# Linear attention and a gated MLP on one core: every SBUF tile moved by 32 bytes

## The chip, the core and the metric

The kernel runs on one core of one Trainium2 chip. The metric is the device time of one execution in microseconds; the time before the change is the median of three runs, 1343.54 us (1341.47 to 1345.01). One further execution was taken with the hardware profiler, and all trace numbers come from it. "PE" is TensorE's matmul stream, "PEld" the loading of its stationary operand, DVE is VectorE, ACT is ScalarE, POOL is GpSimd, and SP is the queue that starts most DMAs.

## The reference

```python
def phi(x):                                   # q, k, v: (8, 8, 576, 64); w_phi: (64, 128)
    proj = np.einsum('bhsd,df->bhsf', x, w_phi)
    proj = proj - np.max(np.abs(proj), axis=-1, keepdims=True)
    return np.concatenate([np.exp(proj), np.exp(-proj)], axis=-1)
q_p, k_p = (phi(q), phi(k))
kv = np.einsum('bhsf,bhsd->bhfd', k_p, v)
num = np.einsum('bhsf,bhfd->bhsd', q_p, kv)
den = np.einsum('bhsf,bhf->bhs', q_p, np.sum(k_p, axis=2))[..., None] + 1e-06
x = (num / den).transpose(0, 2, 1, 3).reshape(4608, 512)
xn = x / np.sqrt(np.mean(x * x, axis=-1, keepdims=True) + 1e-06) * rms_g
g = xn @ w_gate                               # w_gate, w_val: (512, 1536)
out = ((g / (1.0 + np.exp(-g))) * (xn @ w_val)) @ w_out     # w_out: (1536, 512)
```

All data are float32.

## The kernel before

Nearly all products are written as three matmuls of a split operand: a tile is rounded to float32r by ScalarE ("high") and the rest is kept in a second float32r tile ("low"), and high by high, high by low and low by high are added in PSUM. One matmul instruction takes a moving operand of N columns (128 partitions by N elements of 4 bytes, from SBUF) and a stationary operand of 128 columns that is loaded ahead of it (PEld). Three stages follow each other:

- **Attention, up to 508 us.** The 32 pairs of heads are worked off in a software pipeline (`front`, `mid`, `back`, `last`). `front` transposes k and q (L298) and projects them (L311 to L313, N = 256, moving `wh` or `wl`); `mid` exponentiates and forms kv (L346, N = 130, moving `vr`; L351, N = 65, moving `vm`; both in plain float32, which the trace shows as two matmuls for each that the code writes); `back` multiplies with the queries (L415, N = 288, moving `qh` or `ql`, 32 x 4 x 6 = 768 matmuls). Tiles `vm` and `vr` exist three times; pair number modulo 3 picks one. Between these, the first 3 of 12 column blocks of gate and value weights are multiplied with blocks of 288 tokens (`fill`, L474, N = 288, moving `xo`, 1152 matmuls), and go on alone until 606 us.
- **Gate and value, 611 to 1067 us.** For 12 blocks of 384 tokens the other 9 column blocks are multiplied (`gv`, L588, N = 384, moving `xb`, 12 x 9 x 24 = 2592 matmuls); L156 and L157 add 24 of the same width for the norm.
- **Output, 1075 to 1340 us.** For 18 groups of 256 tokens, seven products of a Strassen scheme are made (`omm`, L737, N = 256, moving `wh0` to `wh5` and `wl0` to `wl5`, stationary `xo`). A product runs over kp = 0 to 5, with three matmuls each (moving `wh`, `wl`, `wh`): 18 x 7 x 18 = 2268 matmuls.

Pools hand out SBUF from the low end of a partition, or, with `side="right"`, from the high end, and round each tile's size up to a multiple of 32 bytes. Byte addresses within the partition, as the built program has them:

| tiles | operand in | address of the first | modulo 64 |
|---|---|---|---|
| `eps`, `g` (pool `gl`) | - | 16512, 16544 | 0, 32 |
| `one`, `epsd`, `warm`, `ones` (pool `gl`) | L156 (`ones`) | 16576, 16608, 16640, 16672 | 0, 32, 0, 32 |
| `fg0` to `fv1` (wf1) | L474, L588, stationary | 17184 | 32 |
| `xb`, three buffers | L588, moving | 52512, 79136, 91424 | 32 |
| `xo` of `fill` | L474, moving | 153120, 162336 | 32 |
| `qh`, `ql` | L415, moving | 177696, 196128 | 32 |
| `wh`, `wl` | L311 to L313, moving | 135008, 136032 | 32 |
| `vm0`, `vm1`, `vm2` | L351, moving | 137056, 139136, 141216 | 32, 0, 32 |
| `vr0`, `vr1`, `vr2` | L346, moving | 143296, 143840, 144384 | 0, 32, 0 |
| `wh0` to `wl3` (pool `rg`, right side) | L737, moving | 172000 | 32 |
| `wh4` to `wl5` (pool `owp`, left side) | L737, moving | 113440 | 32 |
| `xo` of `operands` | L737, stationary | 64288 and 15 more | 32 |

All other tiles that TensorE reads (weights, `kt`, `qt`, `th`, `tl`, `er`, `ek`, `yk`, `yq`, `kv`, `ident`) also start at 32 modulo 64. Within a tile the slices that are passed to TensorE are multiples of 64 bytes apart, with `vm` and `vr` as the exception: the 65 columns of `vm` are 260 bytes apart.

The Tile framework sets the order of the instructions on each engine from the order in the code and its own estimates; all five engines run their rows in that order and wait on semaphores.

Of the kernel before, what the change touches and what calls it, by code (L numbers as in the profile page):

```python
# [8 lines left out]
F32 = mybir.dt.float32  # L9
# [73 lines left out]
def kernel(ctx: ExitStack, tc: tile.TileContext, q, k, v, w_phi,  # L83
# [29 lines left out]
    gl = ctx.enter_context(tc.tile_pool(name="gl", bufs=1))  # L113
# [3 lines left out]

    x_ctx = ExitStack()  # L120
    wfp = x_ctx.enter_context(tc.tile_pool(name="wfp", bufs=1))
    wf1 = [[wfp.tile([128, NC, J1 * 128], F32R, name=f"f{n}{i}") for i in range(2)] for n in "gv"]
# [678 lines left out]
```

## Time and profile before

| | |
|---|---|
| median of three runs | 1343.54 us |
| lowest and highest | 1341.47, 1345.01 us |
| span of the profiled execution, first to last instruction | 1345.4 us |
| matmuls in it | 9396 |
| TensorE waits in it for other work, longest sum by line | 9.8 us (L474 for DVE) |

The profiled execution's span lies 1.9 us above the median and 0.4 us above the slowest of the three runs. In the profile a row such as "2.24 PE L588 MATMUL ... x12" is a run of 12 like instructions, with the time from the first one's start to the last one's end. Matmuls overlap at their ends, so the pace of a stream is read from the starts of two runs that follow each other, not from the duration of one.

### The profile page before, as it was taken

To read this page: it belongs to the slowest core of one execution; us is meant where nothing else is said; L and a number is where in the kernel's file an instruction comes from. 1 tells how busy PE (TensorE), PEld (TensorE's weight loads), DVE (VectorE), ACT (ScalarE), POOL (GpSimd) and SP (SyncE) were. 2 spreads that over 40 slices of the span, in tenths; PEclk is the share of its full clock that TensorE was granted. 3 is DMA by queue.
4 is the path that set the end of the run, shared out by engine and by line. 5 is a ranking of instruction groups with operands and counts; after the bars stand their busy time and mean duration, and the time that the engine had idled before them with its cause. 6 is when DMAs were issued, how large, how long until landed. Compare 5 with 4: busy or idle time off the path is not lost.

```text
span 1345.4 us, 25468 instructions
## 1 busy us (share of the span) xinstructions
PE 1291.3 (96%) x9396; PEld 1275.3 (95%) x9396; DVE 914.7 (68%) x1301; ACT 710.0 (53%) x1510; POOL 619.6 (46%) x568
## 2 busy tenths in 40 slices
PE   7989999999999997998999999999999799999998
PEld 7889899999999887998999999999999799999998
DVE  7899888778778762114566656655343489999995
ACT  5988877778778772334434434443332234344332
POOL 3766565555556660000223222222221078878885
PEclk9999999999999898999999999999999999999999
DMA  5455656565556434437454454454333434454351
GB/s 162 125 144 158 162 159 166 168 170 167 161 151 162 125 113 144 150 128 203 145 171 145 157 176 154 133 169 151 110 123 100 158 116 136 132 172 137 126 176 60
DMA packets 204523, 197.21 MB, mean 147 GB/s; under 512 B 69553, under 2 KB 186417, under 8 KB 204401
## 3 DMA queue, kind: packets, MB, share of 16 engines
q1 hardware_dynamic: 194896, 190.88, 47.0%
q10 hardware_dynamic: 9504, 4.72, 1.2%
q8 instruction: 74, 1.21, 0.4%
q14 instruction: 49, 0.39, 0.1%
HBM read 126.04 MB, written 69.50 MB: 145 GB/s over the span
## 4 chain that ended last, share of the span: by engine, by line
PE 80%; DVE 7%; DMA 5%; ACT 4%; issue 2%; POOL 2%; SPq 0%; ACTq 0%; DVEq 0%; POOLq 0%
PE fp L588 15%; PE gp L588 15%; PE fp L474 10%; PE acc L351 6%; PE gd L737 5%; PE gz L737 5%; PE gy L737 5%; PE sm L415 3%; PE fp L737 2%; PE pp L311 2%; PE fp L415 2%; PE pp L313 2%; PE pp L312 2%; PE sm L298 2%; PE sm L364 2%
## 5 line engine op out<-in xcount | busy, mean ns | idle before, releaser
L380 POOL TENSOR_TENSOR ql<-eq,qh 128x256 fp32r<-128x256 f32 x256 | 217.1, 879 | 67.2 <-issue 38.2
L61 POOL TENSOR_TENSOR xo<-st,xo 128x768 fp32r<-128x768 f32 x54 | 125.0, 2328 | 94.0 <-ACT xo L60 92.2
L588 PE MATMUL fp<-xb,wg 128*128 128x384 f32 x864 | 163.0, 336 | 4.6 <-ACT wg L60 4.6
L588 PE MATMUL gp<-xb,wv 128*128 128x384 f32 x864 | 161.5, 334 | 0.0
L588 PEld LDWEIGHTS fp<-xb,wg 128*128 128x128 f32 x864 | 151.9, 189 | 5.1 <-ACT wg L60 4.9
L573 DVE TENSOR_TENSOR h<-sl,gp 128x384 f32<-128x384 f32 x108 | 59.5, 551 | 135.0 <-PE gp L588 71.2
L588 PEld LDWEIGHTS gp<-xb,wv 128*128 128x128 f32 x864 | 150.8, 188 | 0.0
L571 ACT ACTIVATE sl<-fp 128x384 f32<-128x384 f32 x108 | 52.7, 489 | 167.4 <-PE fp L588 148.6
L54 POOL TENSOR_TENSOR wa<-raw,wa 128x192 f32<-128x192 f32 (+1 forms) x112 | 67.4, 622 | 159.5 <-issue 56.7
L351 PE MATMUL acc<-vm,ek 128*128 128x65 f32 x1024 | 131.6, 271 | 0.0
L315 DVE TENSOR_REDUCE mx<-pp 128x4 f32<-128x512 f32 (+1 forms) x160 | 100.5, 631 | 42.4 <-PE pp L313 41.1
L351 PEld LDWEIGHTS acc<-vm,ek 128*128 128x128 f32 x1024 | 127.8, 194 | 0.3 <-ACT ek L338 0.2
L60 ACT CAST xo<-st 128x768 fp32r<-128x768 f32 x54 | 43.4, 835 | 153.1 <-DVE st L675 76.9
L61 POOL TENSOR_TENSOR xb<-x,xb 128x1536 fp32r<-128x1536 f32 x12 | 42.7, 3562 | 152.0 <-ACT xb L60 152.0
L151 POOL TENSOR_TENSOR ss<-ss,sq 128x384 f32<-128x384 f32 x36 | 37.5, 1041 | 154.4 <-ACT sq L150 154.4
L474 PE MATMUL fp<-xo,fg 128*128 128x288 f32 x576 | 95.9, 303 | 9.8 <-DVE xo L61 9.8
L376 ACT ACTIVATE qh<-sm 128x512 fp32r<-128x512 f32 (+1 forms) x192 | 97.1, 506 | 0.0
L474 PEld LDWEIGHTS fp<-xo,fg 128*128 128x128 f32 x576 | 81.8, 190 | 13.2 <-DVE xo L61 12.2
L474 PE MATMUL fp<-xo,fv 128*128 128x288 f32 x576 | 92.5, 299 | 0.0
L61 POOL TENSOR_TENSOR xo<-ht,xo 128x768 fp32r<-128x768 f32 x36 | 91.6, 2545 | 0.0
L311 PE MATMUL pp<-wh,th 128*128 128x256 f32 x288 | 88.6, 309 | 2.7 <-DVE yr L318 2.1
L375 ACT ACTIVATE eq<-sm 128x512 f32<-128x512 f32 x128 | 78.2, 611 | 13.1 <-PE sm L364 12.0
(163 smaller groups left out, 3589.1 us busy)
## 6 DMA issues: line engine op xcount, KB each, us to landing
hs<-h SPq DMA_DIRECT2D x144, 192.0 KB
ht<-hs SPq DMA_DIRECT2D x18, 1536.0 KB
gvs<-fo SPq DMA_DIRECT2D x96, 144.0 KB
gvr<-gvs SPq DMA_DIRECT2D x36, 384.0 KB
rc<-di SPq DMA_DIRECT2D x32, 288.0 KB
x<-xs SPq DMA_DIRECT2D x16, 576.0 KB
x<-xs SPq DMA_DIRECT2D x12, 768.0 KB
kt<-in_k_dram SPq DMA_DIRECT2D x32, 256.0 KB
```

Of the source, the lines that this page charges most:

```text
L54: nc.gpsimd.tensor_tensor(a[:, h], lf[:, h], a[:, h], ALU.mult)
L61: (lo_eng or nc.vector).tensor_tensor(lo, x, hi.bitcast(F32), ALU.subtract)
L311: nc.tensor.matmul(o, th[:, cs], wh, start=True, stop=False)
L315: nc.vector.tensor_reduce(mx[:, 0:2 * m], pp[:, 0:2 * m], axis=AX.X, op=ALU.max, apply_absolute_value=True)
L351: nc.tensor.matmul(acc[:, sg, h], e[h][:, sg, j], vm[:, h, j], start=False, stop=(h == 1 and j == T0 - 1))
L375: nc.scalar.activation(ei[:, sg], yi, AF.Exp, scale=1.0 - 2.0 * sg)
L376: nc.scalar.activation(hi[:, sg], yi, AF.Exp, scale=1.0 - 2.0 * sg)
L380: nc.gpsimd.tensor_tensor(lo[:, sg, cs], ei[:, sg, cs], hi[:, sg, cs].bitcast(F32), ALU.subtract)
L415: nc.tensor.matmul(o[:, 0:SH], a[:, h, sg], e[:, sg, h, cs], start=(i == 0), stop=(i == 5))
L474: nc.tensor.matmul(fp[:, 0:TF], w, xx[x][:, c], start=(i == 0), stop=(i == 3 * NC - 1))
L588: nc.tensor.matmul(gp[:, 0:T], w, e[:, c], start=(i == 0), stop=(i == 3 * NC - 1))
L737: nc.tensor.matmul(place[n], a[:, kp], w[:, o], start=(first and kp == 0 and i == 0), stop=(kp == KP - 1 and i == 2), skip_group_check=True)
```

## The change

Three lines are added after the first tiles of pool `gl`. A tile of 128 x 8 float32 is 32 bytes in each partition. The first call moves everything that the left side hands out later up by 32 bytes; the other two open a pool on the right side ahead of `rg`, and move everything there down by 32 bytes. The two new tiles are never written or read.

```diff
     g = gl.tile([128, NC], F32, name="g")
+    gl.tile([128, 8], F32, name="shift")
+    rsh = ctx.enter_context(tc.tile_pool(name="rsh", bufs=1, side="right"))
+    rsh.tile([128, 8], F32, name="shift")
     x_ctx = ExitStack()
     wfp = x_ctx.enter_context(tc.tile_pool(name="wfp", bufs=1))
```

Each engine has the same instructions in the same order, with the same waits, as before; only addresses differ. Left-hand tiles go up by 32 (`fg0` 17184 to 17216, `xb` 52512 to 52544, `wh4` 113440 to 113472), right-hand ones down by 32 (`wh0` 172000 to 171968). All tiles at 32 modulo 64 come to lie at 0, and the few at 0 (`vm1`, `vr0`, `vr2`; and `one`, `warm` and one buffer of `mx`, which TensorE does not read) at 32. `eps` and `g` stay where they were. DRAM addresses of the inputs and scratch tensors are not touched by the new lines.

## The prediction

> **What bounds the kernel.** I read the page's busy shares first, then the chain of work that ended last, then three stretches, one from each stage.
>
> ```profile
> span 1345.4 us, 25468 instructions
> PE 1291.3 (96%) x9396; PEld 1275.3 (95%) x9396; DVE 914.7 (68%) x1301; ACT 710.0 (53%) x1510; POOL 619.6 (46%) x568
> PEclk9999999999999898999999999999999999999999
> PE 80%; DVE 7%; DMA 5%; ACT 4%; issue 2%; POOL 2%; SPq 0%; ACTq 0%; DVEq 0%; POOLq 0%
> ```
>
> TensorE is busy for 96% of the span, it is 80% of the chain that ended last, and its clock is granted in full in nearly every slice. By stretch (busy us of each engine, then clock, DMA share and GB/s):
>
> ```profile
> core 0: us, PE busy (x) PEld busy (x) DVE busy (x) ACT busy (x) POOL busy (x), PEclk, DMA share, GB/s
> 200.00:400.00 200.00, 198.82 (x1646) 198.04 (x1645) 156.39 (x270) 152.83 (x382) 110.65 (x135) 1.00 0.60 166
> 700.00:800.00 100.00, 100.00 (x579) 100.00 (x578) 63.87 (x99) 42.14 (x74) 26.72 (x27) 1.00 0.50 157
> 1200.00:1300.00 100.00, 100.00 (x868) 100.00 (x867) 95.56 (x71) 39.57 (x58) 85.33 (x36) 1.00 0.46 148
> ```
>
> In each stage TensorE has no gap to speak of: 1.2 us of 200 in attention, none in the other two. So a change of TensorE's pace goes into the time nearly one for one, in both directions. The others have room (DVE at most 156 of 200 in attention, 64 of 100 in gate and value) except in the output stage, where DVE is busy for 95.56 of 100 us: TensorE cannot gain much over 4% there before DVE is the limit.
>
> The change adds no instruction, wait or transfer and moves none. What can differ is how long an instruction takes at its new address. So the sum has three parts: TensorE's pace at a start of 0 instead of 32 modulo 64; its pace where the distance between the two operands changes; and the other engines and DMAs.
>
> **1. The pace of the wide matmuls.** The starts of runs that follow each other, gate-and-value first, then `fill`:
>
> ```profile
> 699.68 2.24 PE L588 MATMUL gp<-xb,wv 128*128 128x384 f32 x12
> 701.76 2.24 PE L588 MATMUL fp<-xb,wg 128*128 128x384 f32 x12
> ...
> 570.15 1.76 PE L474 MATMUL fp<-xo,fv 128*128 128x288 f32 x12
> 571.75 1.76 PE L474 MATMUL fp<-xo,fg 128*128 128x288 f32 x12
> ```
>
> With N = 384, twelve take 701.76 - 699.68 = 2.08 us, 173.3 ns each. With N = 288 they take 1.60 us, 133.3 each. The difference of 40.0 ns for 96 columns is 0.417 ns for a column; by that the columns alone take 160.0 and 120.0 ns, and **13.3 ns** remain in both that do not depend on N. 16 columns take 6.67 ns, and 16 float32 are 64 bytes. If the remainder is two pieces of 64 bytes, one of them the piece that a start in the middle of 64 bytes adds (1536 bytes from offset 32 touch 25 such pieces, from offset 0 only 24), an aligned start saves 6.67 ns. If it is the change from one set of weights to the next, or loading and streaming getting in each other's way, it stays. No operand of a wide matmul starts at 0 now, so no row decides this directly; the bounds are zero and the whole remainder.
>
> How many there are: 2592 + 24 with N = 384, and 1152 + 768 with N = 288, 4536 in all. At nothing: 0. At one piece: 4536 x 6.67 ns = 30.3 us. At the whole remainder: 4536 x 13.3 = 60.5 us.
>
> The nearest row where offsets differ is in attention. `vm0` lies at 32 modulo 64 and `vm1` at 0, so by their pair numbers these two runs, with `vr` ahead of each, read the moving operand at both:
>
> ```profile
> 322.41 0.44 PE L346 MATMUL acc<-vr,er 128*128 128x130 f32 x2
> 322.69 1.90 PE L351 MATMUL acc<-vm,ek 128*128 128x65 f32 x16
> 324.42 0.39 PE L298 MATMUL sm<-ident,kt 128*128 128x128 f32 x2
> ...
> 433.56 0.44 PE L346 MATMUL acc<-vr,er 128*128 128x130 f32 x2
> 433.84 1.90 PE L351 MATMUL acc<-vm,ek 128*128 128x65 f32 x16
> 435.57 0.39 PE L298 MATMUL sm<-ident,kt 128*128 128x128 f32 x2
> ```
>
> The first is a pair with `vm0`, the second one with `vm1`: 324.42 - 322.69 and 435.57 - 433.84 are both 1.73 us, 108 ns a matmul, and `vr0` and `vr1` show 0.44 alike. So an aligned start gains nothing measurable there. The row is not strong: 65 columns are short beside 108 ns, which makes the loading of the weights the limit, and the stationary operands are at 32 in both. It does price the few tiles that go the other way (`vm1`, `vr0`, `vr2`) at nothing. I take 0 for the first part, and keep 30 us as the price of the rival.
>
> The Trainium skill speaks to both sides. Its page "SBUF — State Buffer" (Specifications) gives lines of 16 bytes; 32 modulo 64 is a line's start as much as 0 is, so by that rule the shift saves nothing, in agreement with the `vm` rows. Its page "TensorE: Matmul & The Clock Gate" (Back-to-back issue gap) gives N / 2.4 + 2.5 ns for a warm isolated stream, 162.5 for N = 384, where this trace has 173.3; if all that lies above the rule came from the offset, an estimate by that page is 10.8 ns x 4536 = 49 us.
>
> **2. The distance between the operands in the output stage.** Nearly all tiles move up together, so the distance between a matmul's moving operand and the weights loaded beside it stays. It changes in one place: `wh0` to `wl3` go down by 32 while the stationary `xo` go up by 32. Before, these are at 224 and `xo` at 32 modulo 256, 192 apart; after, 128 apart. `wh4` to `wl5` are 0 apart before and after. That this can matter is in the rows of the output stage (one product of 18, then the start of the next):
>
> ```profile
> 1201.52 0.28 PE L737 MATMUL gz<-wl,xo 128*128 128x256 f32 x1
> ...
> 1202.19 0.28 PE L737 MATMUL gz<-wl,xo 128*128 128x256 f32 x1
> ...
> 1202.54 0.27 PE L737 MATMUL gz<-wl,xo 128*128 128x256 f32 x1
> ...
> 1203.24 0.28 PE L737 MATMUL gz<-wl,xo 128*128 128x256 f32 x1
> ...
> 1113.60 4.16 PE gz L737 x36
> 1117.76 4.41 PE gd L737 x36
> ```
>
> Every third matmul reads a `wl`. From that of kp = 1 to that of kp = 3 (1201.52 to 1202.19) six matmuls, all with right-hand tiles, take 0.67 us, 112 ns each; from kp = 4 to kp = 0 of the next product (1202.54 to 1203.24) six, nearly all with left-hand tiles, take 0.70, 117 each. Size, type and stage are the same, so some address pattern above 64 bytes is worth 4 to 5 ns of a matmul. The last two rows come from the chain of waits: two products are 4.16 us to the next row, 115.6 ns a matmul on average.
>
> The right-hand matmuls are 18 x 7 x 12 = 1512. If all fall to 117 ns, that costs up to 1512 x 5 ns = 7.6 us; since the first of a product are slower than 112 already, I price it at 6 us. If the left-hand ones' slowness is not a matter of distance, it costs 0. If 128 were better than 192 it could gain, but 112 is near the 108 at which loading alone runs in the rows above: at most 1512 x 4 = 6 us. No row has 128 apart with N = 256. I take 0, between the two ends, and keep both.
>
> **3. The others.** DVE, ACT, POOL and the DMAs also get new addresses. In gate and value DVE could slow by half before it bound (63.87 of 100); in the output stage, at 95.56, it could slow by 4%. If that cover went, each further per cent of DVE there would cost about 2.7 us (1% of the stage's 266 us). No row says that they would be slower or faster: 0, both ways.
>
> **The sum.** 0 + 0 + 0 against the profiled execution's 1345.4 us; that lies 1.9 us above the median of the runs shown, so the prediction is made for the median: **1343.5 us**. With the small terms of part 2 in both directions the likeliest case alone spans 1338 to 1348.
>
> **Rivals.**
> - *A start at 64 bytes saves a piece.* Price 30 us, time 1343.5 - 30 = 1313; with something from the 256-wide matmuls as well (2268 of the output stage from 115.6 to at best 112, 8 us, which DVE's share allows) about 1305; at half the price 1328. For it speaks that the remainder is the same 13.3 ns in two widths and just 32 columns long, twice 64 bytes, while every operand starts mid-piece. Against it speak the `vm` rows, and that a change of weights would give the same constant. At the whole remainder 1283.
> - *Slower through the distance.* The mechanism of part 2 in the output stage: 1343.5 + 6 = about 1350; it becomes visible once the 1512 right-hand matmuls lose over 2.7 ns each (4 us). For it: 112 beside 117 ns. Against it: the wide matmuls show one pace although the blocks of `xo` in `fill` lie at four distances from their weights. The same page on TensorE (Step-by-step) says that moving operand and weights have two independent read ports, by which distance could not matter; the 0.67 beside 0.70 us here leaves that open.
> - *The change does not do what it says.* Three moving tiles do end off 64 bytes, against the words of the change, which the `vm` rows price at nothing; the time would again be 1343.5. This is inside the forecast.
>
> **How the numbers follow.** Two medians within 0.3% (4 us) can't be told apart here. Forecast 0.53 (all the same), the saved piece 0.31 (all faster), the distance 0.13 (slower); 0.03 remain for other engines' addresses, slower too. So faster 0.31, same 0.53, slower 0.16. The range goes down to 1309, which takes in the saved piece at its price and leaves out 0.08 for larger savings, and up to 1352, past the distance's price, leaving out 0.05.
>
> **What would show it.** In the changed profile the starts of the L588 runs of 12 decide part 1: 2.08 us apart if the forecast holds, 2.00 if a piece is saved, 1.92 if the whole remainder is; in `fill` 1.60, 1.52 or 1.44. Part 2 shows in the six L737 matmuls from kp = 1 to kp = 3: 0.67 as now, 0.70 or more if distance costs. Part 3 shows in the mean of DVE's and POOL's groups. The forecast is wrong if the first pair of rows moves at all.

## The result, and the profile after

The changed kernel takes 1354.26 us (median of 6 runs, 1348.59 to 1355.11) beside 1345.22 us for the kernel before in its now 6 runs. The ratio of the two, over all these runs, is 1.0054 with a 95% interval of 1.0029 to 1.0079: **slower by about 7 us** (4 to 11); the two medians alone lie 9.0 us apart. The page of the changed kernel, and its three stretches with the columns of the prediction's (line numbers are higher by 3: L591 was L588, L477 was L474, L740 was L737):

```profile
span 1352.9 us, 25468 instructions
PE 1302.3 (96%) x9396; PEld 1287.1 (95%) x9396; DVE 904.8 (67%) x1301; ACT 714.0 (53%) x1510; POOL 619.0 (46%) x568
PEclk9999999999999898999999999999999999999999
PE 80%; DVE 7%; DMA 6%; ACT 3%; issue 2%; POOL 1%; SPq 1%; ACTq 0%; DVEq 0%; POOLq 0%
```

```profile
200.00:400.00 200.00, 198.79 (x1647) 198.02 (x1646) 155.98 (x267) 153.27 (x383) 109.77 (x134) 1.00 0.59 164
700.00:800.00 100.00, 100.00 (x579) 100.00 (x578) 62.46 (x97) 42.19 (x74) 26.70 (x27) 1.00 0.49 154
1200.00:1300.00 100.00, 100.00 (x845) 100.00 (x844) 92.51 (x71) 41.27 (x56) 84.31 (x37) 1.00 0.45 148
```

The number behind TensorE's busy time counts its matmuls. In 100 us of gate and value there are 579, as before; in 200 us of attention 1647 (before 1646). In 100 us of the output stage there are **845, before 868**: 118.3 ns each instead of 115.2, with TensorE busy and its clock full. (The count takes in two or three matmuls that reach over the ends of the stretch; by the starts alone it is 118.7 instead of 115.6.) The starts of the runs of 12 show that the wide matmuls kept their pace:

```profile
698.95 2.24 PE L591 MATMUL fp<-xb,wg 128*128 128x384 f32 x12
701.03 2.24 PE L591 MATMUL gp<-xb,wv 128*128 128x384 f32 x12
...
571.25 1.76 PE L477 MATMUL fp<-xo,fv 128*128 128x288 f32 x12
572.85 1.76 PE L477 MATMUL fp<-xo,fg 128*128 128x288 f32 x12
```

2.08 and 1.60 us, as before. The six matmuls that the prediction named as the sign for the distance did change:

```profile
1203.11 0.28 PE L740 MATMUL gy<-wl,xo 128*128 128x256 f32 x1
...
1203.82 0.28 PE L740 MATMUL gy<-wl,xo 128*128 128x256 f32 x1
...
1204.18 0.28 PE L740 MATMUL gy<-wl,xo 128*128 128x256 f32 x1
...
1204.89 0.28 PE L740 MATMUL gz<-wl,xo 128*128 128x256 f32 x1
```

From kp = 1 to kp = 3 they take 0.71 us instead of 0.67, and from kp = 4 to kp = 0 of the next product 0.71 instead of 0.70: there is no fast group left. The output stage by its first and last matmul (the view of one line: durations, then first and last start), before and after:

```profile
L737 PE MATMUL gd<-wh,xo x432: 276/277/394, 1085.1 to 1340.3; 128*128 128x256 f32 x144
L737 PE MATMUL fp<-wh,xo x216: 276/277/583, 1074.5 to 1327.8; 128*128 128x256 f32 x108
```

```profile
L740 PE MATMUL gd<-wh,xo x432: 274/282/388, 1086.7 to 1347.8; 128*128 128x256 f32 x144
L740 PE MATMUL fp<-wh,xo x216: 274/282/580, 1076.0 to 1335.0; 128*128 128x256 f32 x108
```

By the trace's starts in ns it took 265.7 us before and 271.8 after: 6.1 of the 7.5 us by which the span grew. The other 1.4 came before 1076; four executions of one code (e5 and e7 below) start this stage up to 3.4 us apart. Sorted by moving tile, with the mean gap to the next start (gaps over 140 ns left out), the trace gives:

| moving tile | distance, before | ns | distance, after | ns |
|---|---|---|---|---|
| `wh0` to `wl3` (1512) | 192 | 114.5 | 128 | 118.7 |
| `wh4` to `wl5` (756) | 0 | 117.7 | 0 | 118.7 |

1512 x 4.2 ns are 6.4 us. The left-hand tiles, whose distance did not change, lose 1.0 ns too (0.8 us); gaps of over 140 ns, nearly all at the stage's start, are 21 instead of 27 and give about as much back. This is the place and nearly the price of the second rival; what the distance does, and whether alignment has a part in it, the runs below ask. "Distance" always means the address of the moving operand minus that of the weights, modulo 512 bytes: the prediction counted modulo 256, which gives the same 192, 128 and 0 here.

### The profile page after: what moved, and what is told of

Its sections match the earlier page's. It is cut to its first block, busy times and chain, and to the rows that moved or that the text cites. A ratio compares the mean times of both kernels' runs of the same rounds, so it can differ in the third digit from the quotient of the medians.

```text
span 1352.9 us, 25468 instructions
## 1 busy us (share of the span) xinstructions
PE 1302.3 (96%) x9396; PEld 1287.1 (95%) x9396; DVE 904.8 (67%) x1301; ACT 714.0 (53%) x1510; POOL 619.0 (46%) x568
## 4 chain that ended last, share of the span: by engine, by line
PE 80%; DVE 7%; DMA 6%; ACT 3%; issue 2%; POOL 1%; SPq 1%; ACTq 0%; DVEq 0%; POOLq 0%
PE fp L591 15%; PE gp L591 15%; PE fp L477 10%; PE gd L740 6%; PE gz L740 5%; PE gy L740 5%; PE acc L354 5%; PE sm L418 3%; PE fp L740 3%; PE pp L314 2%; PE pp L316 2%; PE fp L418 2%; PE pp L315 2%; PE sm L301 2%; PE sm L367 2%
## 5 line engine op out<-in xcount | busy, mean ns | idle before, releaser
L61 POOL TENSOR_TENSOR xo<-st,xo 128x768 fp32r<-128x768 f32 x54 | 124.9, 2324 | 97.1 <-ACT xo L60 95.1
L591 PE MATMUL fp<-xb,wg 128*128 128x384 f32 x864 | 163.4, 336 | 4.5 <-ACT wg L60 4.3
L591 PE MATMUL gp<-xb,wv 128*128 128x384 f32 x864 | 161.7, 334 | 0.0
L591 PEld LDWEIGHTS fp<-xb,wg 128*128 128x128 f32 x864 | 151.9, 189 | 5.3 <-ACT wg L60 4.6
L591 PEld LDWEIGHTS gp<-xb,wv 128*128 128x128 f32 x864 | 151.1, 188 | 0.0
L477 PE MATMUL fp<-xo,fg 128*128 128x288 f32 x576 | 97.9, 308 | 8.4 <-DVE xo L61 8.4
L477 PEld LDWEIGHTS fp<-xo,fg 128*128 128x128 f32 x576 | 83.7, 194 | 11.5 <-DVE xo L61 10.7
L477 PE MATMUL fp<-xo,fv 128*128 128x288 f32 x576 | 92.7, 299 | 0.0
L61 POOL TENSOR_TENSOR xo<-ht,xo 128x768 fp32r<-128x768 f32 x36 | 88.7, 2465 | 0.3 <-ACT xo L60 0.3
```

The costliest lines, as they stand in the source:

```text
L61: (lo_eng or nc.vector).tensor_tensor(lo, x, hi.bitcast(F32), ALU.subtract)
L477: nc.tensor.matmul(fp[:, 0:TF], w, xx[x][:, c], start=(i == 0), stop=(i == 3 * NC - 1))
L591: nc.tensor.matmul(gp[:, 0:T], w, e[:, c], start=(i == 0), stop=(i == 3 * NC - 1))
```

## The experiments

Each is the kernel before with pads (tiles that are never used and only move what is handed out after them), unless said otherwise. In the diffs, `...` stands for what is left out of a line, and the line that opens the pool `rsh`, as in the change, is left out too. The rates are matmuls in the stretch from 1200 to 1300 us of its profile (before 868, after 845); paces are means over the starts, as in the table.

**Alignment or distance.** One side moved alone; then all aligned at the old distance.

```diff
 e1   +    gl.tile([128, 8], F32, name="shift")
 e2   +    rsh.tile([128, 8], F32, name="shift")
 e3   +    gl.tile([128, 8], F32, name="shift")
 e3   +    rsh.tile([128, 120], F32, name="shift")
```

> Only the left-hand tiles go up by 32; wh0 to wl3 stay. Their distance to the stationary xo becomes 160 modulo 512 (before 192, changed kernel 128), their own start stays 480 modulo 512, and every left-hand operand starts at 0 modulo 64. Theory 'distance': the 1512 right-hand matmuls of the output stage take the same pace as in e2_right_only, whatever it is, between 114 and 119 ns; total 1345 to 1352 us. Rival 'place of the moving operand': 114 ns as before, 1345 us. Rival 'start at 0 modulo 64 is slow': mixed, left-hand tiles of the output stage and all of attention slower, 1350 us.

> Only the right-hand tiles go down by 32; distance 160 modulo 512 as in e1_left_only, moving start 448 modulo 512 as in the changed kernel, stationary xo at 288 as before. Theory 'distance': the same pace as e1_left_only to 1 ns. Rival 'place of the moving operand': 118.7 ns as in the changed kernel, 1351 us or more, while e1_left_only has 114.

> All TensorE operands that the change aligns are at multiples of 64 bytes as in the changed kernel (left-hand tiles up by 32), but the right-hand tiles go down by 480 instead of 32, so that their distance to xo is 192 modulo 512 as before. Theory 'distance': right-hand matmuls back at 114.4 ns, output stage back at 266 us, total as before (1345 us, ratio 1.000 to 1.002). Rival 'alignment to 64 itself costs': 118.7 ns and 1354 us as in the changed kernel, ratio 1.005. If the matmuls are back at 114 but the time is not, something else at the new addresses costs 2 to 3 us.

Measured: e1 1352.53 us, ratio 1.0051 (1.0032 to 1.0070), 843 matmuls; e2 1352.38, ratio 1.0053 (1.0032 to 1.0074), 844 matmuls; e3 **1344.83, ratio 0.9994 (0.9980 to 1.0009)**, 867 matmuls, output stage 265.7 us.

```profile
1200.00:1300.00 100.00, 100.00 (x843) 100.00 (x842) 97.96 (x72) 39.62 (x56) 87.25 (x36) 1.00 0.45 148
```

```profile
1200.00:1300.00 100.00, 100.00 (x844) 100.00 (x842) 97.89 (x72) 40.24 (x56) 87.25 (x36) 1.00 0.46 148
```

```profile
1200.00:1300.00 100.00, 100.00 (x867) 100.00 (x867) 97.74 (x73) 39.49 (x56) 87.25 (x36) 1.00 0.46 148
```

These are e1, e2, e3. e1 and e2 move different operands to one distance, 160, and agree: the medians are 0.15 us apart and the right-hand tiles at 118.4 ns in both. With the weights in their old place (e2) or the right-hand tiles in theirs (e1) the loss is there all the same, so neither place decides it. e3 has every alignment of the changed kernel and none of its loss. So a start at 64 bytes has no effect that these runs can tell (0.2%), and the changed distance carries the loss.

**A distance for all, and a map.** Pads ahead of `wh4` (and ahead of the projection's `wh` in e4) bring all 256-wide matmuls to 192; m1 to m3 set three distances each, e6 all to 320.

```diff
 e4 e5 +    owp.tile([128, 48], F32, name="pad")
 e4    +    const.tile([128, 32], ...); wh = ...; wl = ...; const.tile([128, 96], ...)
 m1    +    rsh.tile([128, 120], ...); owp.tile([128, 80], ...); pool.tile([128, 120], ...) if kp == 2
 m2    +    rsh.tile([128, 80], ...); owp.tile([128, 16], ...); pool.tile([128, 112], ...) if kp == 2
 m3    +    rsh.tile([128, 40], ...); owp.tile([128, 72], ...); pool.tile([128, 112], ...) if kp == 2
 e6    +    rsh.tile([128, 96], ...); owp.tile([128, 80], ...)
```

> Starts from the kernel before: nothing is aligned, but 192 bytes ahead of wh4 and 128 bytes ahead of the projection's wh bring all moving operands with 256 columns to a distance of 192 modulo 512 from their weights. Theory 'distance': the 756 left-hand matmuls of the output stage fall from 117.8 to 113.5 ns (3.3 us), the slow start of each product goes too (0.5 us or more), and the 864 of the projection fall from 117 to 113.5 where they follow each other (up to 3 us); total 3 to 7 us faster, 1338 to 1342 us. Rival 'left and right side differ as such': both stay, 1345 us.

> Only the 192 bytes ahead of wh4: the left-hand moving tiles of the output stage come to distance 192, attention and gate-and-value keep every address. Theory 'the attention addresses of e4 cost what its output stage gained': output stage 261.6 us as in e4 and the rest as before, total 1341 us, ratio 0.997. Rival 'the 4 us of the output stage do not reach the total, or runs scatter by as much': ratio 1.000 again.

> A map of distances modulo 512 in the output stage: kp 0 and 1 at 256, kp 2 and 3 at 224, kp 4 and 5 at 320. Theory 'one narrow good distance': 224 near 192 in place but all three at 117 to 119 ns. Rival 'half of the distances are good': 224 and 256 at 113.5, 320 slow.

> kp 0 and 1 at 448, kp 2 and 3 at 384, kp 4 and 5 at 64. If the pattern repeats every 256 bytes, 448 is as good as 192 (113.5 ns) and 384 as bad as 128 (118.7); if it repeats every 512 or not at all, 448 is slow like the others. 64 is the distance of the projection's wh and should show about 117.

> kp 0 and 1 at 96, kp 2 and 3 at 32, kp 4 and 5 at 288. With a period of 256, 32 and 288 show the same pace; 96 lies beside 128 and should be slow, 117 to 119 ns, in each case.

> All moving tiles of the output stage at distance 320 modulo 512 from the weights, the other distance that the map showed at 113.4 ns. Theory 'each good distance gives 113.4 ns to a stream of its own kind': output stage 261 to 262 us in the profile. For the total, theory 'two paces at one distance': single runs fall into two groups about 9 us apart, near 1342 and near 1351, as those of e5_output_192 did (seven from 1339.7 to 1344.3, five from 1350.1 to 1353.6). Rival 'ordinary scatter of attention': one group around 1343.

e4: 1346.11, ratio 1.0003 (0.9982 to 1.0023), though its output stage was 261.6 us in the profile, 4 less; the projection stayed at about 117 ns a matmul, so being at 192 did not make it fast. e5: 1344.14, ratio 1.0002 (0.9980 to 1.0025), output stage again 261.6 us and 885 matmuls. Its 12 runs lie in two groups: seven from 1339.7 to 1344.3 and five from 1350.1 to 1353.6. Half of the expectation failed: the profile gained, the total did not.

m1 to m3 ran once each: 1345.45 (m1), 1353.69 (m2) and 1354.18 us (m3). In them 32, 64, 96, 224, 256, 288, 384 and 448 ran at 117 to 121 ns by tile, and 320 at 113.3. (448, which would be as good as 192 if the pattern repeated every 256 bytes, ran at 117 to 118.) That reads as two good distances, 192 and 320, and e6 refutes the reading: with 320 for all, the profile has 852 matmuls in 100 us, 117.8 ns in nearly every product. Its runs are at 1348.11, ratio 1.0029 (1.0013 to 1.0045), spread from 1345.6 to 1353.3: neither the two groups nor the one near 1343 that had been expected. So the distance of a tile alone does not give its pace; what ran just before it seems to count too, and the map says less than it seems to.

**The two groups.** The code of e5 ran and was profiled three times more.

> The same code as e5_output_192, profiled once more. Theory 'two paces': a profile with a span of about 1349 us shows an output stage of 270 us or a part of it at 117 to 119 ns a matmul with unchanged addresses; one of about 1340 shows 261.6. Rival: in a long profile the output stage is 261.6 and attention or gate and value is longer.

> As e7_again_a: a further execution of the same code, to meet both groups.

> As e7_again_a: a further execution of the same code, to meet both groups.

1340.82, 1352.70 and 1349.65 us; output stages of 261.6, 270.0 and 269.9 us by the starts, and the same addresses throughout. The short executions have the short stage and the long ones the long one, 8.3 to 8.4 us apart. The rows of e5 and e7_again_b from 1200 to 1300 us:

```profile
1200.00:1300.00 100.00, 100.00 (x885) 100.00 (x884) 94.98 (x71) 39.31 (x56) 87.23 (x37) 1.00 0.46 148
1200.00:1300.00 100.00, 100.00 (x852) 100.00 (x851) 97.83 (x72) 40.85 (x56) 86.97 (x36) 1.00 0.46 148
```

e7_again_c changed its pace within the execution (TensorE alone, idle time ahead of it in brackets):

```profile
1116.43 0.28 PE L737 MATMUL gd<-wl,xo 128*128 128x256 f32 x1
...
1117.45 0.28 PE L737 MATMUL gd<-wl,xo 128*128 128x256 f32 x1
1117.91 0.50 PE L737 MATMUL gd<-wh,xo 128*128 128x256 f32 x2 [0.18 <-POOL xo L61]
...
1118.60 0.28 PE L737 MATMUL gd<-wl,xo 128*128 128x256 f32 x1
...
1119.66 0.28 PE L737 MATMUL gd<-wl,xo 128*128 128x256 f32 x1
```

Nine matmuls from 1116.43 to 1117.45 take 1.02 us, 113.3 ns each. Then TensorE waits once for POOL, and nine from 1118.60 to 1119.66 take 1.06 us, 117.8 each; by the starts every later product stays at 117.8. At this distance, 192, the stream has **two paces, and in these profiles holds the one it has until it stalls**. A stall need not change it: e7_again_a, after stalls at the same places, went on at 113.3, and e7_again_c itself had kept 113.3 through earlier ones. It can also change back: e4's profile, at 192 too, went to 117.8 at a stall near 1090 us and returned to 113.3 at one near 1105.

**Is 128 slow in itself?** All tiles at one distance, 128 or 0, and then 192 with kp = 5 alone at 0.

```diff
 g1 +    rsh.tile([128, 16], ...); owp.tile([128, 32], ...)
 g2 +    rsh.tile([128, 48], ...)
 g3 +    owp.tile([128, 48], ...); pool.tile([128, 80], ...) if kp == 5
```

> All moving tiles of the output stage at distance 128 from the weights. (a) '128 is slow in itself': every product at 117 ns or more, output stage 270 us. (b) 'two paces at any distance': stretches at 113.3 ns between stalls of TensorE, in this or the second profile.

> A second profile of g1_all_128, since (b) leaves the choice of pace to each stall.

> All moving tiles of the output stage at distance 0. (a) every product at 117.8 ns, as the left-hand ones of the kernel before; (b) stretches at 113.3.

> kp 0 to 4 at distance 192, kp 5 alone at 0. Theory 'the change of distance sets the stream back to the fast pace in each product': 15 of 18 matmuls at 113.4 apart from one of 123, in every product of the profile; output stage 263 to 264 us; single runs in one group, total 1342 to 1343 us, ratio 0.998. Rival 'the pace is kept from stall to stall whatever the distances': whole stretches at 117.8, and runs in two groups up to 8 us apart as in e5_output_192.

```profile
1200.00:1300.00 100.00, 100.00 (x845) 100.00 (x844) 92.12 (x71) 40.99 (x54) 83.37 (x36) 1.00 0.45 148
```

```profile
1200.00:1300.00 100.00, 100.00 (x835) 100.00 (x834) 87.20 (x71) 39.75 (x52) 80.72 (x35) 1.00 0.45 148
```

```profile
1200.00:1300.00 100.00, 100.00 (x836) 100.00 (x835) 87.18 (x69) 40.92 (x54) 81.73 (x35) 1.00 0.45 148
```

These are g1 (1349.81 us), its repeat (1354.70) and g2 (1351.04), with output stages of 271.8, 274.5 and 274.8 us. By the starts, 128 gives 118.7 in one execution. The other began there and went to 120.0 at about 1088 us, again two paces, but here without a stall: no matmul near that time starts more than 122 ns after the one before it. 0 gives 120.0 in every product after the first, more than the 117.8 that was expected from the left-hand tiles of the kernel before. Neither shows a stretch at 113.3. So reading (a) holds as far as these three executions go: **the distance bears on which paces there are, and 128 and 0 showed no fast one**. g3 has 876 matmuls and a stage of 263.6 us; every product after the first few of its profile ran its kp = 1 to 4 at 113 to 114. Its runs are one group, 1342.57 to 1347.05, median 1345.87, ratio 0.9993 (0.9979 to 1.0007): the stage and the single group came as expected, the total of 1342 to 1343 did not. That agrees with the change of distance as a reset to the fast pace, which is not shown further. The kernel before and e3 have such a change in each product too, and their right-hand tiles are at 114.5 on average in both profiles.

**Is it the same cost in the wide matmuls?** h1 brings the moving operands with 384 columns from distance 0 to 192.

```diff
 h1 +    xops[0].tile([128, 48], ...); xips[0].tile([128, 80], ...)
 h1 +    xops[1].tile([128, 48], ...); const.tile([128, 80], ...)      # const of gate and value
```

> The 2592 matmuls with 384 columns at distance 192 instead of 0 from their weights (four pads of 192 or 320 bytes around the buffers of xb), the rest as in the kernel before. Theory 'the 13.3 ns above the columns' time are what the distance costs': 166.7 ns a matmul at the best, gate and value 17 us shorter, 1328 us. Rival 'a fixed cost that a stream with 384 columns pays at each distance', as the 288-wide ones do at four distances: 173.3 ns and 1345 us.

The pace stayed at 173.3 ns, with 579 matmuls from 700 to 800 us: the rival held. The median is 1349.74 us, ratio 1.0029 (1.0005 to 1.0052), but the profiled execution has a span of only 1344.4 us and shows no loss; what made other runs of it longer stays open. No version beats the kernel before by more than the measurement can tell.

## Why the prediction was wrong

- **What bounds the kernel.** Right: the loss in TensorE's pace went into the time nearly whole, 6.1 us in the stage of the 7.5 in the span.
- **Part 1, the wide matmuls at a start of 0 modulo 64.** Right. 2.08 and 1.60 us stayed as they were, and e3 leaves at most 0.2% for alignment of everything. The 13.3 ns are not a piece of 64 bytes and, by h1, for 384 columns not the distance either; what they are stays open. The prediction took these rows alone as what would prove it wrong; they did not move, and it was wrong by its other sign. The Trainium skill's page "SBUF — State Buffer" (Specifications), with lines of 16 bytes, gave this outcome and the trace agrees (2.08 and 1.60 us unchanged). What lies above the N / 2.4 + 2.5 ns that the Trainium skill's page "TensorE: Matmul & The Clock Gate" (Back-to-back issue gap) gives for isolated matmuls is still unexplained (173.3 beside 162.5 ns for 384 columns).
- **Part 2, the distance. This step failed.** It had the right operands, place and count, bounds from a gain of 6 us to a loss of 7.6, and then took "0, between the two ends". The term was 1512 x 4.2 = 6.4 us. The trace of before leaned one way: within the output stage the tiles at 192 were at 113 to 114 after the first few of a product, and those at 0 at 117. A third distance was in the trace too, 64 in the projection, at about 117 by the starts, a row that the prediction did not look at; e4 showed later that the projection stays there at 192 as well, so that row alone proves little. Still, the only fast matmuls were at the distance that the change took away, and a new one was better taken near 117 than near 112. What held me back, that the wide matmuls show one pace at four distances, holds for 288 columns (h1 adds 192 beside 0 for 384), but did not carry over to 256.
- **The price of part 2.** The 6 us came close in part by luck. The 112 ns was read from two stamps of 10 ns; by the trace's starts in ns these six matmuls take 113.3 each, and all the right-hand ones 114.5, while after the change they are at 118.7 and not at 117. Both ends were too low, by 2.5 and 1.7 ns, so most of the error cancelled.
- **The rule against it.** The Trainium skill's page "TensorE: Matmul & The Clock Gate" (Step-by-step) says that the two operands have independent read ports, so that loading weights does not slow the running matmul. The prediction concluded that distance could not matter. e3 differs from the changed kernel in the place of the right-hand tiles alone, e1 and e2 show that neither operand's place decides it by itself, and the change of distance is worth 0.5% of the kernel: the measurement decides against this conclusion. Whether the ports are what the two operands meet at is not shown.
- **Part 3, the other engines.** Right as to the time: the trace shows nothing else that slowed TensorE. POOL's `xo<-st,xo` group has a mean of 2324 ns in the changed kernel, 4 less than before. DVE's `xo<-ht,xo` did move, from 1665 to 1480 ns, which is faster; why is not shown.
- **Rival two's time.** 1350 was priced from a median of 1343.54; the kernel before is at 1345.22 over 6 runs, to which 6.4 adds up to 1351.6. The rest to 1354.26 is within the interval of the ratio. The upper end of the range, 1352, took in the mechanism but not the scatter of either median.

That 256 columns are sensitive and 288 or 384 are not fits their own time. At 0.417 ns a column, 256 columns take 106.7 ns, about as long as the 108 at which the 65-column matmuls of the prediction's rows follow each other, where it took the loading of weights as the limit; 120 and 160 ns leave slack. This is argued, not shown.

## What to carry to other kernels

A change of allocation can change the distance between operands; before a tile is aligned, list which pairs of TensorE operands keep their distance and which don't, above all pairs from opposite ends of SBUF. Where the matmuls of one line read tiles from different places, read the pace by moving tile rather than by line: one mean of 115.6 ns hid a fast and a slow group. Where a trace shows one fast group and a change takes away what sets it apart, do not price that at nothing because the sign is unsure. And if a code's runs fall into two groups, profile it more than once before believing a gain of one profile.

## What the runs showed of the hardware that was not expected

With 256 float32r columns and the whole output stage at one distance, the pace stood at a few fixed values: 113.3 and 117.8 ns at distance 192, 117.8 at 320, 118.7 and 120.0 at 128, 120.0 at 0. 120.0 is the columns' 106.7 plus the same 13.3 ns that the wide matmuls show, and 113.3 is 106.7 plus half of it. At 192 one code ran at either value, kept it for over 200 us, and changed it only at a stall; this makes the stage 8.3 to 8.4 us longer in one execution than in another, and the medians of e5's two groups of runs lie 8.5 us apart. At 128 the value also changed without a stall, once. What sets the value is open.
